# A channel-attention and FFN kernel: held subtractions of low halves, other rooms, and a tenth tile on seven products

## The chip, the cores and the metric

One core of a Trainium2 chip runs the whole program. The metric is the device time of one execution in microseconds (us); the times of several executions are given as a median with the lowest and the highest.

## What is computed

The reference attends over channels and then applies a two-layer network to every token.

```python
B, N, C = 4, 6080, 256            # d_model 256, d_ff 2048, 24320 tokens
qn = q / (norm(q, axis=1) + 1e-06)
kn = k / (norm(k, axis=1) + 1e-06)
s = kn.transpose(0, 2, 1) @ qn / tau
a = softmax(s)                    # over the last axis, 256 x 256 for each batch
x = (v @ a).reshape(B * N, C)
h = x @ w_in
g = maximum(0.01 * h, h)
out = g @ w_out
```

## The kernel before

**Tiles and slots.** For each batch the kernel multiplies the 256 x 256 attention matrix into `w_in` once, so that a token needs two projections: v by that product (256 to 2048), the leaky unit, and `w_out` (2048 to 256). The tokens are cut into 24 tiles of 2 x 512 or 2 x 496 tokens, six for each of four batches, and the 2048 hidden channels into eight pairs of 128-channel blocks. A tile and a pair make a slot, written (tile, pair) here: 192 slots, run one after the other by the loop over `i` and `p` at the end of the program. Operands are split into a high and a low half (float16 from tile 6 on); a product is three matmuls, or passes: high by high, low weight by high, high weight by low.

**The first projection** uses seven block products in place of eight (`block_product`, L1188, 21 matmuls in each slot, L1193). They accumulate in two PSUM banks, `ps_x` and `ps_z`. ScalarE copies partial sums out of `ps_x` (`taken`, tile `h`, L1239) or into `ps_z` (`seed`, L1228), and VectorE adds a copy to what stands in `ps_z` (`add`, tile `h`, L1233). The last product into `ps_x` waits for the copy `h22`, and the last into `ps_z` for VectorE's sum `h22`.

**The leaky unit** (`leaky`, L1199) works on the four blocks C11, C22, C21 and C12 of a slot. ScalarE writes the result in float32 (tile `g`, L1207) and its high half (tile `g_split`, L1207 or L1214); VectorE then subtracts the one from the other for the low half (L1218). C12 of a slot is handled at the start of the next one (`last`).

**The second projection** of a plain tile (`ffn_out`, L1598, matmuls at L1613) is a generator of 24 matmuls a pair: four blocks, two halves of the output, three passes. It runs one slot later, a few matmuls at a time: `out(6)`, `out(5)`, `out(7)` and `out(24)` fill the places in which TensorE would wait. After the last pair the four output banks are copied (L1630 on ScalarE, L1634 on VectorE) and stored.

**Fast tiles.** From tile 15 on (`FAST`, which `EARLY = 3` sets) a slot is written by `fast_slot` (L1514), and the second projection uses seven products as well: 21 matmuls a pair (`fast_out`, L1339). The sums of blocks that this needs are made by accumulating DMAs on POOL's queue (`sums_start`, L1305), the sums of `w_out` beforehand by VectorE (`wo_sums`, started in the slots of `SUMS_AT`). The first fast tile has its own rooms (`front` and `end`).

**Order of the rest.** All other work stands in queues (`todo`): splitting v for the next tile (`v_split`), squares and norms of q and k, scaled q and k (`unit` by VectorE, their high half `qk_split` by ScalarE, L362), the softmax, and the products and splits of the next batch's weights (`w_first`, `w_rest`, which POOL's queue stores). `slot(queue, room)` issues entries at its place until their lengths, constants in the code, fill the room. So the order on every engine is fixed when the program is built, and each engine runs it in order. A few lines of a plain slot show the places:

```python
                slot("dve", 2.1)
                block_product(i, p, x, S2, "T2", False, False)
                h12 = leaky(i, p, "C11", z if h11 is None else h11, lambda: taken(i, x))
                slot("dve", 2.2)
                slot("act", 1.8)
                out(5)
                block_product(i, p, z, S1, "T1", True, False)
                slot("pe", 1)
...
            block_product(i, p, x, S3, "T3", False, False)
            h22 = taken(i, x)
            add(i, h22, z)
```

Of the kernel before, what the change touches and what calls it, by code (L numbers as in the profile page):

```python
# [30 lines left out]
RBUFS = 4  # L31
RSQRT_MAGIC = float(0x5F3759DF)
TOP = 12
SUMS_AT = (79, 110, 113, 121)
UNITS = 5
SCORES_AT = {1: (8, 20), 2: (48, 22), 3: (0, 0)}
NORMS_AT = 80
G_SCALE = 2.0**-19
G_LESS = 2.0**-2
EARLY = 3  # L40


@with_exitstack
def channel_attention_ffn(
# [17 lines left out]
    nc = tc.nc  # L62
# [1133 lines left out]
                )  # L1196
        issued["pe"] = mm

    def leaky(i, p, name, h, then=None):  # L1199

        n = widths[i % NT]
        out = work.tile([P, TW], F32, name="g", bufs=3)
        sp = work.tile([P, 2, TW], pair_type(i), name="g_split", bufs=GBUFS)
        g_split[i, p, name] = sp

        def unit(to):
            return nc.scalar.activation(  # L1207
                out=to, in_=h[:, 0:n], func=AF.Prelu, alpha=0.01, scale=G_SCALE if i >= T16 else 1.0
            )

        run("act", unit, out[:, 0:n])
        between = then() if then else None
        if name == "C21" or then:
            run("act", lambda: nc.scalar.copy(out=sp[:, 0, 0:n], in_=out[:, 0:n]))  # L1214
        else:
            run("act", unit, sp[:, 0, 0:n])
        with in_order("dve"):
            issued["dve"] = nc.vector.tensor_tensor(  # L1218
                out=sp[:, 1, 0:n], in0=out[:, 0:n], in1=f32(sp[:, 0, 0:n]), op=ALU.subtract
            )  # L1220
        return between

    def seed(i, p, x, z):

# [373 lines left out]
    def ffn_out(i, p):  # L1598

        b, t = divmod(i, NT)  # L1600
        n = widths[t]
        f2 = (p // 2) * FPC + p % 2
        f1 = f2 + 2
        assert {f2 // FPB, f1 // FPB} <= wo_done
        if p == 0:
            o_ps[i] = [[bank("o", 4) for _ in range(CH)] for _ in range(2)]
        for name, f, j in (("C11", f1, 0), ("C22", f2, 1), ("C21", f2, 0), ("C12", f1, 1)):
            sp = g_split.pop((i, p, name))
            early = name in ("C11", "C22")
            for h in range(CH):  # L1610
                for k, (x, y) in enumerate(((0, 0), (1, 0), (0, 1))):
                    with in_order("pe"):
                        issued["pe"] = nc.tensor.matmul(  # L1613
                            out=o_ps[i][j][h][:, 0:n],
                            lhsT=wo_lhsT(i, x, f, h),
                            rhs=sp[:, y, 0:n],
                            start=p == 0 and early and k == 0,
                            stop=p == NPAIR - 1 and not early and k == 2,
                        )
                    yield  # L1620
            if p == NPAIR - 1 and not early:
                n0 = b * N + begins[t] + j * n
                act, dve = (nc.scalar.copy, nc.scalar), (nc.vector.tensor_copy, nc.sync)
                parts = [(0, 0, n, act[0], nc.sync), (1, 0, n, *dve)]
                for h, a, z, copy, queue in parts:
                    o = work.tile([P, TW], F32, name="o_sb", tag="temp", bufs=TEMPS)
                    if i < T16:
                        copy(out=o[:, a:z], in_=o_ps[i][j][h][:, a:z])
                    elif copy is act[0]:
                        nc.scalar.activation(  # L1630
                            out=o[:, a:z], in_=o_ps[i][j][h][:, a:z], func=AF.Copy, scale=v_scale[i].out
                        )
                    else:
                        nc.vector.tensor_scalar(  # L1634
                            out=o[:, a:z], in0=o_ps[i][j][h][:, a:z], scalar1=v_scale[i].out, scalar2=None,
                            op0=ALU.mult,
                        )
                    queue.dma_start(out=outT[h * P:(h + 1) * P, n0 + a:n0 + z], in_=o[:, a:z])

# [797 lines left out]
    for i in range(NTILES):  # L2439
        for p in range(NPAIR):  # L2440
# [17 lines left out]
            h11 = seed(i, p, x, y) if seeded else taken(i, x)  # L2458
            if seeded:
                z = y  # L2460
                if last is not None:
                    leaky(*last)
                    last = None
                slot("act", 0.65)
                slot("act_late", 0.65)
                out(6)
                slot("pe", 1 if len(todo["pe"]) < 2 else 3)
                block_product(i, p, z, A12, "B21", h11 is not None, True)
                if h11 is not None:
                    add(i, h11, z)  # L2470
                slot("dve", 2.1)
                block_product(i, p, x, S2, "T2", False, False)
                h12 = leaky(i, p, "C11", z if h11 is None else h11, lambda: taken(i, x))
                slot("dve", 2.2)
                slot("act", 1.8)
                out(5)
                block_product(i, p, z, S1, "T1", True, False)
                slot("pe", 1)
            else:
                block_product(i, p, y, A12, "B21", True, True)  # L2480
                slot("act", 0.65 if i else 0.75 if p else 1.5)
                slot("act_late", 0.65)
                add(i, h11, y)
                if last is not None:
                    leaky(*last)
                    last = None
                slot("dve", 1.45 if i else 1.3)
                out(5)
                slot("pe", 1 if i and len(todo["pe"]) < 2 else 3)
                if i:  # L2490
                    leaky(i, p, "C11", h11)
                slot("dve", 2.2 if i else 2.6 if p < NPAIR - 1 else 1.5)
                block_product(i, p, x, S2, "T2", False, False)
                h12 = taken(i, x)
                if i == 0:
                    leaky(i, p, "C11", h11)
                    slot("dve", 1.0)
                if i:
# [3 lines that stand above are left out]
                slot("pe", 1 if i or p else 2)  # L2502
# [2 lines left out]
            add(i, h22, z)  # L2505
            if i == 0:
                slot("act", 2.2)
            slot("dve", 1.45 if i else 2.8)
            out(7 if seeded else 8)
            slot("act_first", 0.65)  # L2510
# [2 lines left out]
            if i == 0:  # L2513
                slot("act", 0.6)
            else:
                leaky(i, p, "C22", h22)
            block_product(i, p, x, A22, "T4", False, True)
            block_product(i, p, z, S4, "B22", False, True)
            add(i, h12, z)
            leaky(i, p, "C21", x)  # L2520
            slot("act", 0.65 if i else 0.75)
            slot("act_late", 0.65)
            slot("dve", 0.8)
            if i == 0:
                leaky(i, p, "C22", h22)
                slot("dve", 1.5)
            if i == 0 and p < NPAIR - 1 or seeded and (i, p) != (FAST[0] - 1, NPAIR - 1):
                last = i, p, "C12", h12
            else:
                leaky(i, p, "C12", h12)  # L2530
            out(24)
            outs.append(ffn_out(i, p))
    while outs:
        out(24)
    fast_finish()
# [30 lines left out]
```

## Time and profile before

| | |
|---|---|
| median of 3 runs | 2066.24 us (2065.58 to 2069.65) |
| profiled execution, its own time | 2066.94 us |
| its span, first to last instruction | 2065.2 us |
| TensorE matmuls | 2037.5 us busy, 99% of the span, 9522 instructions |
| VectorE | 1658.5 us, 80%, 3077 instructions |
| ScalarE | 1547.5 us, 75%, 2866 instructions |
| GpSimd (POOL) | 338.2 us, 16%, 431 instructions |
| SyncE's DMA queue | 218.61 MB; GpSimd's DMA queue 112.29 MB |

Busy time is the time in which an engine runs at least one instruction. Matmuls are pipelined: each is shown with its own duration, longer than the distance to the next one. Idle time is put down to the instruction or the DMA that ended it. Tiles are found in the trace by the matmuls of L1193, 21 to a slot: tile 3 starts at 342.92 us, tile 13 at 1233.87, tile 14 at 1323.81, tile 15 at 1406.26, tile 16 at 1473.11, tile 17 at 1543.88, and the last slot at 2038.41.

### The profile page before, as it was taken

The page shows a single profiled execution, that of the slowest core. Times are in us where ns is not written, and L with a number is a line of the kernel's source. Part 1 is how long each engine was busy: PE and PEld are TensorE (multiplying, and loading weights), DVE is VectorE, ACT ScalarE, POOL GpSimd, SP SyncE. Part 2 cuts the span into 40 slices and gives each one's busy share as a digit, 9 for nine tenths or more (in the row PEclk, how much of TensorE's full clock was granted, in tenths as well). Part 3 has the DMA queues.
Part 4 walks back from the last instruction along what each step waited for, and adds up shares of the span by engine and source line. Part 5 has one row for each costly group of instructions (what it writes and reads, how often), then busy time and mean ns, then how long its engine had stood idle before and what let it go on. Part 6 is the DMA issues. An engine that isn't in the chain of part 4 may idle for free.

```text
span 2065.2 us, 27833 instructions
## 1 busy us (share of the span) xinstructions
PE 2037.5 (99%) x9522; PEld 1180.9 (57%) x9522; DVE 1658.5 (80%) x3077; ACT 1547.5 (75%) x2866; POOL 338.2 (16%) x431
## 2 busy tenths in 40 slices
PE   9999999999999999999999999999999999999999
PEld 8888887888874545444454554444444444444444
DVE  8987788776767787778787776877989889988976
ACT  6577777765567888877676666767988888898886
POOL 0000000000001222111010000102433333333342
PEclk9999999999999999999999999999999999999999
DMA  9945577445745877534233322213768876876774
GB/s 368 395 169 202 198 242 233 164 165 171 231 155 184 262 191 200 153 95 124 89 128 109 124 63 63 107 37 82 148 141 175 173 160 130 164 143 140 143 134 94
DMA packets 146815, 332.88 MB, mean 161 GB/s; under 512 B 16848, under 2 KB 48336, under 8 KB 146672
## 3 DMA queue, kind: packets, MB, share of 16 engines
q1 hardware_dynamic: 92912, 218.61, 31.3%
q0 software_dynamic: 53536, 112.29, 27.0%
q8 instruction: 75, 1.23, 0.2%
q14 instruction: 68, 0.56, 0.1%
q10 hardware_dynamic: 224, 0.20, 0.0%
HBM read 188.74 MB, written 57.42 MB: 119 GB/s over the span
## 4 chain that ended last, share of the span: by engine, by line
PE 87%; DVE 6%; ACT 4%; issue 2%; DMA 1%; POOL 0%; SPq 0%; ACTq 0%; POOLq 0%
PE ps_o L1613 25%; PE ps_x L1193 21%; PE ps_z L1193 16%; PE ps_o L1339 10%; PE ps_s L404 4%; PE ps_s L1339 2%; PE ps_y L1339 2%; PE ps_o L404 2%; DVE g_split L1218 1%; DVE h L1233 1%; PE ps_s L1965 1%; ACT g_split L1214 1%; PE ps_y L404 1%; ACT h L1239 1%; DVE v_split L1139 1%
## 5 line engine op out<-in xcount | busy, mean ns | idle before, releaser
L1613 PE MATMUL ps_o<-g_split,w_out_split 128*128 128x512 f16 (+3 forms) x2880 | 709.2, 382 | 0.2 <-ACT o_sb L1630 0.2
L1193 PE MATMUL ps_x<-v_split,w_split 128*128 128x512 f16 (+3 forms) x2280 | 619.7, 380 | 9.2 <-ACT h L1239 7.8
L1218 DVE TENSOR_TENSOR g_split<-g,g_split 128x512 f16<-128x512 f32 (+3 forms) x480 | 328.2, 684 | 239.4 <-ACT g_split L1207 171.6
L1193 PEld LDWEIGHTS <-w_split 128*128 128x128 f16 x3024 | 293.1, 98 | 367.3 <-issue 35.0
L1193 PE MATMUL ps_z<-v_split,w_split 128*128 128x512 f16 (+3 forms) x1704 | 463.3, 380 | 12.0 <-DVE h L1233 9.0
L1233 DVE TENSOR_TENSOR h<-ps_z,h 128x512 f32<-128x512 f32 (+1 forms) x387 | 263.8, 682 | 73.6 <-ACT h L1239 62.6
L1239 ACT COPY h<-ps_x 128x512 f32<-128x512 f32 (+1 forms) x395 | 229.0, 580 | 102.5 <-PE ps_x L1193 92.2
L1613 PEld LDWEIGHTS <-w_out_split 128*128 128x128 f16 x1728 | 168.9, 98 | 202.1 <-issue 1.0
L1207 ACT ACTIVATE g<-h 128x512 f32<-128x512 f32 (+1 forms) x250 | 156.9, 627 | 119.9 <-DVE h L1233 119.8
L1613 PEld LDWEIGHTS ps_o<-g_split,w_out_split 128*128 128x128 f32 x1152 | 216.4, 188 | 43.7
L1298 DVE TENSOR_TENSOR g_pair<-g_b,g_pair 128x512 f16<-128x512 f32 (+1 forms) x214 | 139.2, 678 | 45.9 <-ACT g_pair L1293 45.6
L1339 PE MATMUL ps_o<-g_pair,w_out_split 128*128 128x512 f16 (+1 forms) x630 | 172.8, 376 | 0.4 <-ACT g_pair L1293 0.3
L1207 ACT ACTIVATE g_split<-h 128x512 f16<-128x512 f32 (+3 forms) x248 | 152.2, 614 | 0.0
L1214 ACT CAST g_split<-g 128x512 f16<-128x512 f32 (+3 forms) x232 | 143.1, 617 | 3.7
L1339 PEld LDWEIGHTS <-spare 128*128 128x128 f16 x840 | 82.2, 98 | 96.9 <-issue 0.4
L1293 ACT CAST g_pair<-g_b 128x512 f16<-128x512 f32 (+1 forms) x214 | 123.1, 610 | 0.0
L1193 PEld LDWEIGHTS ps_x<-v_split,w_split 128*128 128x128 f32 x576 | 107.7, 188 | 25.6 <-ACT h L1239 2.7
L1207 ACT ACTIVATE g<-ps_z 128x512 f32<-128x512 f32 (+1 forms) x110 | 65.0, 591 | 64.8 <-PE ps_z L1193 64.3
L1228 ACT COPY ps_z<-ps_x 128x512 f32<-128x512 f32 (+1 forms) x110 | 62.5, 569 | 55.4 <-PE ps_x L1193 45.7
L1339 PEld LDWEIGHTS <-w_out_split 128*128 128x128 f16 x630 | 61.6, 98 | 72.9 <-issue 0.6
L1305 POOL DMA_DIRECT2D g_a<-g_a x70 | 63.3, 905 | 227.7 <-DVE g_pair L1298 140.1
L1298 DVE TENSOR_TENSOR g_pair<-g_a,g_pair 128x512 f16<-128x512 f32 (+1 forms) x144 | 97.2, 676 | 1.5 <-ACT g_pair L1293 1.0
(280 smaller groups left out, 2811.9 us busy)
## 6 DMA issues: line engine op xcount, KB each, us to landing
w_split<-w_dram SPq DMA_DIRECT2D x40, 896.0 KB, 6.9
qk_raw<-in_q_dram SPq DMA_DIRECT2D x115, 256.0 KB, 3.2
qk_raw<-in_k_dram SPq DMA_DIRECT2D x115, 256.0 KB, 5.8
v_raw<-in_vT_dram SPq DMA_DIRECT2D x32, 512.0 KB, 4.1
out_dram<-o_sb SPq DMA_DIRECT2D x64, 256.0 KB, 3.0
w_split<-w_dram SPq DMA_DIRECT2D x32, 448.0 KB, 5.2
spare<-spare POOLq DMA_DIRECT2D x23, 512.0 KB, 5.5
g_a<-g_a POOLq DMA_DIRECT2D x40, 256.0 KB, 3.3
```

Source lines behind the costliest of these rows:

```text
L404: mm = nc.tensor.matmul(out=out, lhsT=lhsT, rhs=rhs, start=start, stop=stop, skip_group_check=True)
L1193: mm = nc.tensor.matmul(out=ps[:, 0:n], lhsT=w[:, x, a, :], rhs=sp[:, y, 0:n], start=first and k == 0, stop=k == 2, skip_group_check=True,)
L1207: return nc.scalar.activation(out=to, in_=h[:, 0:n], func=AF.Prelu, alpha=0.01, scale=G_SCALE if i >= T16 else 1.0)
L1214: run("act", lambda: nc.scalar.copy(out=sp[:, 0, 0:n], in_=out[:, 0:n]))
L1218: issued["dve"] = nc.vector.tensor_tensor(out=sp[:, 1, 0:n], in0=out[:, 0:n], in1=f32(sp[:, 0, 0:n]), op=ALU.subtract)
L1233: issued["dve"] = nc.vector.tensor_tensor(out=h[:, 0:n], in0=ps[:, 0:n], in1=h[:, 0:n], op=ALU.add)
L1239: issued["act"] = nc.scalar.copy(out=h[:, 0:n], in_=ps[:, 0:n])
L1293: return nc.scalar.copy(out=sp[:, 0, 0:n], in_=g32[i, p, HELD.get(name, name)][:, 0:n])
L1298: return nc.vector.tensor_tensor(out=sp[:, 1, 0:n], in0=g32[i, p, HELD.get(name, name)][:, 0:n], in1=sp[:, 0, 0:n], op=ALU.subtract)
L1305: return nc.gpsimd.dma_start(out=g32[i, p, to][:, 0:n], in_=g32[i, p, of][:, 0:n], accum_op=ALU.add)
L1339: issued["pe"] = nc.tensor.matmul(out=ps[:, 0:n], lhsT=fast_lhsT(i, p, prod, x), rhs=sp[:, y, 0:n], start=p == 0 and k == 0, stop=ends and ...
L1613: issued["pe"] = nc.tensor.matmul(out=o_ps[i][j][h][:, 0:n], lhsT=wo_lhsT(i, x, f, h), rhs=sp[:, y, 0:n], start=p == 0 and early and k == ...
```

## The change

`leaky` gets an argument `held`: VectorE's subtraction is then put into a list (`rests`) and issued by `rest_of(n)` at a later place. In plain tiles from tile 1 on, C11's is issued behind the sum `h22`, C22's behind the sum `h12`, C21's at the start of the next slot and C12's behind the product T2 of that next slot. The rooms of a plain slot change: 1.8 to 1.3 and 0.65 to 1.25 for ScalarE, 0.8 to 1.45 for VectorE, and a room of 0.8 more at the end of each tile's first slot. In `ffn_out` the last matmul of a block and what follows it (the output copies) are issued in one step. `EARLY` becomes 4, so that tile 14 is the first fast tile, and three entries of `SUMS_AT` move up by eight slots.

```diff
-SUMS_AT = (79, 110, 113, 121)
+SUMS_AT = (79, 102, 105, 113)
...
-EARLY = 3
+EARLY = 4
...
-    def leaky(i, p, name, h, then=None):
+    def leaky(i, p, name, h, then=None, held=False):
...
-        with in_order("dve"):
-            issued["dve"] = nc.vector.tensor_tensor(
+        def rest():
+            return nc.vector.tensor_tensor(
                 out=sp[:, 1, 0:n], in0=out[:, 0:n], in1=f32(sp[:, 0, 0:n]), op=ALU.subtract
             )
+
+        if held:
+            rests.append(rest)
+        else:
+            run("dve", rest)
         return between
+
+    rests = []
+
+    def rest_of(n):
+        for _ in range(min(n, len(rests))):
+            run("dve", rests.pop(0))
...
@@ ffn_out
-                    yield
+                    if (h, k) != (CH - 1, 2):
+                        yield
...
                     queue.dma_start(out=outT[h * P:(h + 1) * P, n0 + a:n0 + z], in_=o[:, a:z])
+            yield
...
@@ the loop over slots
             if seeded:
                 z = y
+                rest_of(9 if p == 0 else 1)
                 if last is not None:
-                    leaky(*last)
+                    leaky(*last, held=True)
                     last = None
...
                 block_product(i, p, x, S2, "T2", False, False)
-                h12 = leaky(i, p, "C11", z if h11 is None else h11, lambda: taken(i, x))
+                rest_of(1)
+                h12 = leaky(i, p, "C11", z if h11 is None else h11, lambda: taken(i, x), held=True)
                 slot("dve", 2.2)
-                slot("act", 1.8)
+                slot("act", 1.3)
...
             add(i, h22, z)
             if i == 0:
                 slot("act", 2.2)
+            if seeded:
+                rest_of(9)
             slot("dve", 1.45 if i else 2.8)
...
-                leaky(i, p, "C22", h22)
+                leaky(i, p, "C22", h22, held=True)
             block_product(i, p, x, A22, "T4", False, True)
             block_product(i, p, z, S4, "B22", False, True)
             add(i, h12, z)
-            leaky(i, p, "C21", x)
-            slot("act", 0.65 if i else 0.75)
+            if i and p == 0 and 0.0:
+                pass
+            else:
+                rest_of(9)
+            leaky(i, p, "C21", x, held=i > 0)
+            slot("act", (1.25 if p else 1.25) if i else 0.75)
             slot("act_late", 0.65)
-            slot("dve", 0.8)
+            slot("dve", (1.45 if p else 1.45) if i else 0.8)
...
             else:
+                rest_of(9)
                 leaky(i, p, "C12", h12)
             out(24)
             outs.append(ffn_out(i, p))
+            if i and p == 0:
+                rest_of(9)
+                slot("dve", 0.8)
```

The first place is VectorE in slot (12, 4), from the second subtraction of the slot to the sum `h22` and a little past it. Before (`g_split` with its number names the block: 11481 is C12 of slot (12, 3), 11514 is C11 of this slot):

```order
L1218 TENSOR_TENSOR g_split_11481<-g_11480,g_split_11481 128x512
L1136 TENSOR_SCALAR v_split_11506<-v_raw_10960,v_scale_11145 128x512
L1139 SCALAR_TENSOR_TENSOR v_split_11506<-v_raw_10960,v_scale_11145,v_split_11506 128x512
L1160 TENSOR_TENSOR v_raw_10960<-v_raw_10960 128x512
L1218 TENSOR_TENSOR g_split_11514<-g_11513,g_split_11514 128x512
L1160 TENSOR_TENSOR v_raw_10960<-v_raw_10960 128x512
L366 TENSOR_TENSOR qk_split_11463<-unit_11430,qk_split_11463 128x2x256
L356 TENSOR_TENSOR unit_11522<-qk_raw_11190,spare_5885 128x512
L1233 TENSOR_TENSOR h_11542<-ps_z_11475,h_11542 128x512
L356 TENSOR_TENSOR unit_11545<-qk_raw_11268,spare_5885 128x512
```

The same engine and place in the change (11537 is C21 of slot (12, 3), 11560 its C12, 11593 is C11 of this slot):

```order
L1218 TENSOR_TENSOR g_split_11537<-g_11536,g_split_11537 128x512
L1136 TENSOR_SCALAR v_split_11584<-v_raw_11041,v_scale_11227 128x512
L1139 SCALAR_TENSOR_TENSOR v_split_11584<-v_raw_11041,v_scale_11227,v_split_11584 128x512
L1160 TENSOR_TENSOR v_raw_11041<-v_raw_11041 128x512
L1218 TENSOR_TENSOR g_split_11560<-g_11559,g_split_11560 128x512
L1160 TENSOR_TENSOR v_raw_11041<-v_raw_11041 128x512
L366 TENSOR_TENSOR qk_split_11540<-unit_11509,qk_split_11540 128x2x256
L356 TENSOR_TENSOR unit_11600<-qk_raw_11304,spare_5885 128x512
L1244 TENSOR_TENSOR h_11615<-ps_z_11553,h_11615 128x512
L1218 TENSOR_TENSOR g_split_11593<-g_11592,g_split_11593 128x512
```

The kinds of instructions ahead of the sum (L1233, now L1244) are the same; each subtraction's place is taken by the block before it, and C11's has moved behind the sum.

The second place is VectorE in slot (13, 6), between the first subtraction and the sum `h22`. Before:

```order
L874 SCALAR_TENSOR_TENSOR w_first<-w_s,w_first 128x256 x2
L1218 TENSOR_TENSOR g_split<-g,g_split 128x512
L1975 TENSOR_TENSOR w_c<-w_c,ps_y 128x512
L1136 TENSOR_SCALAR v_split<-v_raw,v_scale 128x512
L1139 SCALAR_TENSOR_TENSOR v_split<-v_raw,v_scale,v_split 128x512
```

And in the change:

```order
L1136 TENSOR_SCALAR v_split<-v_raw,v_scale 128x512
L1139 SCALAR_TENSOR_TENSOR v_split<-v_raw,v_scale,v_split 128x512
L874 SCALAR_TENSOR_TENSOR w_first<-w_c,w_first 128x128
L874 SCALAR_TENSOR_TENSOR w_first<-w_c,w_first 128x256
L1218 TENSOR_TENSOR g_split<-g,g_split 128x512
L874 SCALAR_TENSOR_TENSOR w_first<-w_s,w_first 128x256 x2
```

The splits of the last batch's weights (L874) stand closer here: twelve instructions in the whole slot in place of six. Before, the last of them stood in slot (14, 1).

## Rows read from the trace of the kernel before

**Rows 1.** The page's first part: busy time of each engine.

```profile
PE 2037.5 (99%) x9522; PEld 1180.9 (57%) x9522; DVE 1658.5 (80%) x3077; ACT 1547.5 (75%) x2866; POOL 338.2 (16%) x431
```

**Rows 2.** Busy time by stretch: tiles 3-13, 14, 15, 16, 17 to last slot.

```profile
core 0: us, PE busy (x) PEld busy (x) DVE busy (x) ACT busy (x) POOL busy (x), PEclk, DMA share, GB/s
...
342.92:1323.81 980.89, 964.86 (x4596) 563.11 (x4595) 744.79 (x1407) 699.80 (x1321) 89.92 (x134) 1.00 0.49 149
1323.81:1406.26 82.45, 78.62 (x362) 35.22 (x361) 60.25 (x119) 55.74 (x108) 6.13 (x9) 1.00 0.14 52
1406.26:1473.11 66.85, 65.79 (x298) 28.95 (x297) 56.69 (x108) 56.73 (x104) 21.54 (x25) 1.00 0.63 126
1473.11:1543.88 70.77, 70.77 (x338) 32.87 (x337) 64.17 (x120) 60.99 (x115) 26.76 (x32) 1.00 0.71 138
1543.88:2038.41 494.53, 493.52 (x2314) 226.26 (x2313) 433.04 (x787) 424.61 (x786) 189.54 (x221) 1.00 0.75 150
```

**Rows 3.** Waits of TensorE in tiles 3 to 13: us, times, longest.

```profile
PE ps_x L1193 <- ACT h L1239: 7.4, 8, 1.6
PE ps_z L1193 <- DVE h L1233: 7.4, 17, 1.1
PE ps_x L1193 <- ACT wo L1007: 0.5, 1, 0.5
PE ps_o L1613 <- ACT o_sb L1630: 0.2, 1, 0.2
```

**Rows 4.** Busy time by stretch: slots (7, 4), (7, 5) and (14, 6).

```profile
738.39:749.51 11.12, 11.12 (x54) 5.70 (x53) 9.28 (x16) 9.69 (x19) 2.50 (x4) 1.00 0.55 136
749.51:761.18 11.67, 11.30 (x54) 5.67 (x53) 9.29 (x16) 9.70 (x19) 3.38 (x5) 1.00 0.81 196
...
1386.83:1396.54 9.71, 9.71 (x46) 4.41 (x45) 4.56 (x8) 6.49 (x12) 0.00 (x0) 1.00 0.19 74
```

**Rows 5.** Order of time, TensorE in slot (12, 4): start, duration, instruction, idle before.

```profile
1192.50 0.81 PE L1193 MATMUL ps_z<-v_split,w_split 128*128 128x512 f16 x3
...
1193.79 1.67 PE L1613 MATMUL ps_o<-g_split,w_out_split 128*128 128x512 f16 x7
1196.44 0.81 PE L1193 MATMUL ps_x<-v_split,w_split 128*128 128x512 f16 x3 [0.97 <-ACT h L1239]
...
1197.81 1.46 PE L1613 MATMUL ps_o<-g_split,w_out_split 128*128 128x512 f16 x6
```

**Rows 6.** Order of time, ScalarE in slot (12, 4).

```profile
1195.28 0.62 ACT L362 CAST qk_split<-unit 128x512 f16<-128x512 f32 x1 [2.56 <-DVE unit L356]
1195.81 0.58 ACT L1239 COPY h<-ps_x 128x512 f32<-128x512 f32 x1
```

**Rows 7.** Order of time, VectorE in slots (12, 4) and (12, 5).

```profile
1189.71 0.69 DVE L1218 TENSOR_TENSOR g_split<-g,g_split 128x512 f16<-128x512 f32 x1 [0.64 <-ACT g_split L1207]
...
1192.75 0.69 DVE L1218 TENSOR_TENSOR g_split<-g,g_split 128x512 f16<-128x512 f32 x1 [0.56 <-ACT g_split L1214]
...
1196.42 0.69 DVE L1233 TENSOR_TENSOR h<-ps_z,h 128x512 f32<-128x512 f32 x1 [1.17 <-ACT h L1239]
...
1202.06 0.69 DVE L1218 TENSOR_TENSOR g_split<-g,g_split 128x512 f16<-128x512 f32 x1 [1.25 <-ACT g_split L1207]
...
1204.98 0.69 DVE L1218 TENSOR_TENSOR g_split<-g,g_split 128x512 f16<-128x512 f32 x1 [0.91 <-ACT g_split L1214]
...
1207.98 0.68 DVE L1233 TENSOR_TENSOR h<-ps_z,h 128x512 f32<-128x512 f32 x1
```

**Rows 8.** Waits of VectorE in tiles 3 to 13: us, times, longest.

```profile
DVE g_split L1218 <- ACT g_split L1207: 125.1, 108, 2.4
DVE g_split L1218 <- ACT g_split L1214: 58.8, 63, 3.5
DVE h L1233 <- ACT h L1239: 35.8, 36, 2.1
```

**Rows 9.** Waits of TensorE in tile 14.

```profile
PE ps_z L1193 <- ACT ps_z L1228: 2.4, 1, 2.4
PE ps_z L1193 <- DVE h L1233: 1.4, 3, 0.7
```

**Rows 10.** Order of time, ScalarE in slot (14, 1).

```profile
1337.04 0.61 ACT L862 ACTIVATE w_first<-w_c 128x128 f16<-128x128 f32 x2 [2.57 <-DMA w_dram<-w_first]
```

## The prediction

> **What bounds the kernel now.** I read the page's engine totals first, then the same totals cut into stretches, then TensorE's waits in two of the stretches, then the order of time around one wait. A reader should see five things.
>
> TensorE is busy 99% of the span [rows 1] at a granted clock of 1.00, which is its level of 2.4 GHz [rows 2]. VectorE (80%) and ScalarE (75%) are not far behind. The end is therefore set by TensorE: its work, plus the time that the others make it wait.
>
> The waits lie in a few places [rows 2]. Tiles 3 to 13 take 980.89 us, with TensorE busy 964.86: 16.03 us idle. Tile 14 loses 3.83 us, tile 15 1.06, tile 16 none, and the 494.53 us from tile 17 to the start of the last slot 1.01. In tiles 3 to 13, 17 waits are for VectorE's sum `h` and 8 for ScalarE's copy `h`, with two others: 27 waits, 15.5 us [rows 3].
>
> A wait costs more than its idle time. Two slots of the same matmuls (54 in each) last 11.12 and 11.67 us; the second has only 0.37 us of idle [rows 4]. The other 0.18 us is the draining tail of the matmul before the wait, which counts as busy. So tiles 3 to 13 lose about 16.0 + 27 x 0.18 = 20.9 us. Tile 14 is checked directly: its quiet slots take 9.71 us [rows 4], eight would be 77.7, and it took 82.45: 4.8 us.
>
> The Trainium skill ("Trainium Kernel Development and Optimization", Performance Expectations) says that matmul busy time is a bad measure of the distance to the limit because matmuls are pipelined. The trace agrees: by busy time the two stretches lose 19.9 us, by slot lengths 25.7. The sum below goes by the slot lengths.
>
> Why TensorE waits is seen in slot (12, 4). The last product into `ps_x` waits 0.97 us for ScalarE's copy `h` [rows 5]. ScalarE had stood 2.56 us before that copy, for a `unit` that VectorE makes [rows 6]. VectorE had stood 0.64 and then 0.56 us in front of two subtractions at L1218, whose high half ScalarE had not finished [rows 7]: 1.20 us, against a loss of 0.97 + 0.18. In slot (12, 5) two such stands of 1.25 and 0.91 us come ahead of VectorE's sum at 1207.98 [rows 7]. Over tiles 3 to 13 VectorE stands 183.9 us before such subtractions [rows 8], some 2.1 us in each of 88 slots; what reaches TensorE is a ninth of that.
>
> **The change, part by part.**
>
> *Seven products in tile 14.* The second projection of a fast tile takes 21 matmuls a pair where a plain one takes 24: 24 fewer over eight pairs. Seven matmuls are shown with 1.67 us and three with 0.81 [rows 5], so one more costs 0.215 us: **-5.2 us**, on TensorE itself. ScalarE and VectorE get what before's tile 15 already gives them, and POOL 32 more accumulating DMAs. In the new order tile 14 holds before's tile 15 and tile 15 holds before's tile 16, instruction for instruction on ScalarE and VectorE but for widths and one deferred subtraction. Tile 15 lost 1.06 us of idle with those instructions and tile 16 none, at the same 32 POOL DMAs and VectorE 64.17 us busy of 70.77 [rows 2]. So I charge the new tile 14 with what tile 15 loses now, and the new tile 15 with nothing. What falls out is the plain tile 14 with its waits [rows 9]: **-4.8 us**. Its greatest, 2.4 us, came from ScalarE standing 2.57 us for the DMA that empties a `w_first` buffer [rows 10].
>
> *Held subtractions.* No instruction is added. The number of VectorE instructions ahead of the sum `h22` stays as it was in (12, 4); what changes is which blocks' subtractions stand there. Those of C22, C21 and C12 of the slot before take the places of C21, C12 and this slot's C11, whose high halves ScalarE finishes only just then. The stands go; the work stays. Upper bound of the gain: all 20.9 us. Lower bound: zero, if other stands take their place, and below zero if the subtractions come late (a rival). The row nearest to it is (12, 4), where the stands ahead equal the loss; in (12, 5) they are 2.16 us against a loss near 0.55. But the waits for ScalarE hang on a longer chain, and the softmax and weight steps bring stands of their own. I take three quarters: **-16 us**.
>
> Is a held half late? The shortest lead is C11's: in (12, 4) it would follow the sum of 1196.42 [rows 7] and end near 1197.8. TensorE's third pass over C11 comes in the next slot, after the six matmuls from 1197.81, three of the next product and two passes, near 1200.2 [rows 5]: 2.4 us in hand.
>
> *Rooms and sums.* The rooms move steps between places of the same slot: no count changes, and the price lies in the three quarters. `SUMS_AT` moves three groups of weight sums up by eight slots, and the weight steps of the last batch, which ran in tiles 13 and 14, now end in tile 13. In (13, 6) VectorE gets twelve `w_first` instructions where it had six. Between zero and tile 14's 4.8 us can come back here; I take it as part of the quarter that stays.
>
> *Output copies* stand right behind their last matmul instead of at the next group: one wait of 0.2 us in tiles 3 to 13 [rows 3] can go; counted at nothing.
>
> Sum: -5.2 - 4.8 - 16 = -26.0. The profiled execution took 2066.94 us (span 2065.2 and 1.7 around it), 0.7 above the median of the three runs. 2066.94 - 26.0 = **2041 us**.
>
> **Rivals.**
>
> *ScalarE's chain holds.* If the stands on L1218 only hide ScalarE's own lateness, the eight waits for its copy stay (7.4 + 8 x 0.18 = 8.8 us) and half of the rest: 6 us instead of 16, so 2051. For it: VectorE also stood 35.8 us for that copy [rows 8]. Against: in (12, 4) ScalarE stood for VectorE, not the other way.
>
> *The squeezed steps wait in tile 13.* The `w_first` buffer wait and its neighbours return one tile earlier and take back the 4.8 us: 2046. For it: the wait hangs on buffers that a DMA empties, and the steps are denser. Against: tile 14 held them while its quiet slots left VectorE 4.56 us busy of 9.71 [rows 4], so it was order rather than load that stalled it.
>
> *Late halves (the slower side).* VectorE runs so far behind that TensorE meets held halves unfinished. Each such meeting stops it once a slot; the 104 plain slots of tiles 1 to 13 eat the 26 us at 0.25 us a slot. At 0.3 us it is 2066.94 - 26 + 31 = 2072. It needs VectorE to trail by the 2.4 us lead, which at 744.79 us busy of 980.89 [rows 2] only a few slots could see.
>
> *Blocked POOL DMAs.* If VectorE's instructions held up POOL's issues, tile 14's pair sums would come late. In tile 16 the same mix leaves POOL 26.76 us busy in 32 issues, of 70.77, and TensorE without idle [rows 2]. POOL would set the pace only if each issue's 0.84 us grew by more than 44 / 32 = 1.4 us; at three times the length it would be 80 us, 9.5 more than the tile: 2050.5. Against it stands tile 16 itself. The Trainium skill ("SBUF — State Buffer", SBUF: two separate sides, with the section on the bandwidth pool behind it) states such a lock between VectorE's two-port modes and the descriptors that GpSimd writes: 620 ns for a DMA alone, 3100 ns beside VectorE. An estimate by that page is 2.5 us more for each of 32, and so some 2077 us in all. The trace of tile 16 disagrees with it for this mix.
>
> **How the numbers follow.** Forecast 0.75, ScalarE's chain 0.09, squeezed steps 0.10, late halves 0.05, blocked DMAs 0.01. From no change a measurement tells 0.2%, 4.1 us. All but the late halves are faster, save 0.01 of the squeezed steps (several tiles hit) that ends within 0.2%; late halves near the break-even give another 0.01. That makes 0.94, 0.02, 0.04. The range: with all 20.9 us gone 2036, and 2034 with the small waits outside these tiles as well; upward it takes in 2046 and 2051 and ends at 2053. That leaves out some 0.15.
>
> **What would show it.** TensorE's matmul records fall by 24, and tile 14 is near 67 us with waits like tile 15's. Right: VectorE's idle before the subtraction falls from 183.9 us to a small part in tiles 3 to 13, and TensorE's idle there from 16 to about 4. Wrong: that idle falls but TensorE's stays (ScalarE's chain); waits gather in tile 13 on `w_first` or `ps_z`; the second projection's matmuls `ps_o` wait for `g_split`; or tile 14 shows waits beyond tile 15's.

## The result and the profile after

The changed kernel takes **2034.95 us** (median of 4 runs, 2034.52 to 2035.84); the kernel before took 2067.36 us beside it (4 runs). The ratio is 0.9843, with an interval of 0.9826 to 0.986. The forecast was 2041 us, 2034 to 2053, so the time lies 0.95 us above the lower end of the range. One execution of a kernel below, C11's behind the room, took 7555.62 us where its three others took 2036.05 to 2037.11; it is left out of that kernel's median, and its cause is not known.

The profiled execution of the change took 2034.65 us, its span 2032.8: 32.4 us less than the span of before.

The page's first part answers to [rows 1]. There are 24 matmuls fewer, and every engine's share is higher because the span is shorter:

```profile
PE 2022.6 (99%) x9498; PEld 1180.1 (58%) x9498; DVE 1665.4 (82%) x3115; ACT 1564.8 (77%) x2890; POOL 367.1 (18%) x463
```

The busy time by stretch answers to [rows 2] (same columns): tiles 3 to 13, 14, 15, 16, and 17 to the start of the last slot.

```profile
342.03:1302.32 960.29, 957.19 (x4596) 564.27 (x4595) 746.29 (x1442) 710.02 (x1338) 97.86 (x143) 1.00 0.51 155
1302.32:1369.17 66.85, 65.78 (x298) 28.98 (x297) 57.11 (x109) 56.50 (x104) 21.80 (x25) 1.00 0.62 126
1369.17:1441.70 72.53, 72.53 (x337) 32.84 (x336) 65.22 (x120) 62.38 (x115) 26.56 (x31) 1.00 0.70 137
1441.70:1512.47 70.77, 70.77 (x338) 32.87 (x336) 64.15 (x120) 61.03 (x115) 27.40 (x32) 1.00 0.74 146
1512.47:2006.00 493.53, 493.34 (x2315) 226.19 (x2314) 433.04 (x787) 424.61 (x786) 189.22 (x221) 1.00 0.75 150
```

Set against [rows 2], tiles 3 to 13 give 980.89 - 960.29 = 20.6 us. Tiles 14 and 15 together go from 149.3 to 139.4: 9.9 us. From tile 16 to the last slot it is 1.0 us (565.3 to 564.3). The remaining 0.9 us lies ahead of tile 3, which starts at 342.03 in place of 342.92. The clock is 1.00 in all of them, in both kernels.

What TensorE still waits for in tiles 3 to 13 answers to [rows 3]: 4 waits where there were 27.

```profile
PE ps_x L1193 <- ACT h L1250: 0.9, 1, 0.9
PE ps_y L348 <- DVE n_split L341: 0.8, 1, 0.8
PE ps_z L1193 <- DVE h L1244: 0.7, 1, 0.7
PE ps_z L1193 <- ACT ps_z L1239: 0.6, 1, 0.6
```

VectorE's waits in the same stretch answer to [rows 8]. The 183.9 us before subtractions have become 8.6. VectorE now stands before its sums (L1244, L1233 before), for ScalarE's copy or for TensorE's product, because it comes there early:

```profile
DVE h L1244 <- ACT h L1250: 149.0, 75, 5.0
DVE h L1244 <- PE ps_z L1193: 25.9, 28, 2.5
DVE g_split L1218 <- ACT g_split L1207: 8.6, 9, 1.8
```

Slot (12, 4) shows how, against [rows 5 to 7]. On VectorE the subtraction of C12 starts at once; the step `unit` follows; then the engine stands 1.54 us before the sum `h22`; C11's subtraction comes behind it.

```profile
1175.94 0.68 DVE L1218 TENSOR_TENSOR g_split<-g,g_split 128x512 f16<-128x512 f32 x1
...
1177.74 0.68 DVE L356 TENSOR_TENSOR unit<-qk_raw,spare 128x512 f32<-128x512 f32 x1
1179.97 0.69 DVE L1244 TENSOR_TENSOR h<-ps_z,h 128x512 f32<-128x512 f32 x1 [1.54 <-ACT h L1250]
1180.58 0.68 DVE L1218 TENSOR_TENSOR g_split<-g,g_split 128x512 f16<-128x512 f32 x1
```

ScalarE's cast waits 0.38 us for that `unit`, where it stood 2.56 us before [rows 6], and its copy `h22` now waits for TensorE:

```profile
1178.46 0.62 ACT L362 CAST qk_split<-unit 128x512 f16<-128x512 f32 x1 [0.38 <-DVE unit L356]
1179.35 0.59 ACT L1250 COPY h<-ps_x 128x512 f32<-128x512 f32 x1 [0.27 <-PE ps_x L1193]
```

TensorE goes on to the last product into `ps_x` without a pause, where it lost 0.97 us before [rows 5]:

```profile
1179.15 1.67 PE L1624 MATMUL ps_o<-g_split,w_out_split 128*128 128x512 f16 x7
1180.66 0.81 PE L1193 MATMUL ps_x<-v_split,w_split 128*128 128x512 f16 x3
```

### The profile page after: what moved, and what is told of

Its sections match the earlier page's. It is cut to its first block, busy times and chain, and to the rows that moved or that the text cites. A ratio compares the mean times of both kernels' runs of the same rounds, so it can differ in the third digit from the quotient of the medians.

```text
span 2032.8 us, 27944 instructions
## 1 busy us (share of the span) xinstructions
PE 2022.6 (99%) x9498; PEld 1180.1 (58%) x9498; DVE 1665.4 (82%) x3115; ACT 1564.8 (77%) x2890; POOL 367.1 (18%) x463
## 4 chain that ended last, share of the span: by engine, by line
PE 96%; DVE 2%; DMA 1%; ACT 0%; issue 0%; SPq 0%; DVEq 0%; ACTq 0%; POOLq 0%
PE ps_o L1624 28%; PE ps_x L1193 24%; PE ps_z L1193 18%; PE ps_o L1350 12%; PE ps_s L404 4%; PE ps_y L1350 2%; PE ps_s L1350 2%; PE ps_o L404 2%; PE ps_s L1978 1%; PE ps_y L404 1%; DMA w_dram<-w_first 1%; PE ps_y L1978 0%; PE ps_y L821 0%; PE ps_o L1373 0%; DVE g_split L1218 0%; DVE h L1244 0%
## 5 line engine op out<-in xcount | busy, mean ns | idle before, releaser
L1624 PE MATMUL ps_o<-g_split,w_out_split 128*128 128x512 f16 (+3 forms) x2688 | 661.9, 382 | 0.0
L1244 DVE TENSOR_TENSOR h<-ps_z,h 128x512 f32<-128x512 f32 (+1 forms) x387 | 264.5, 683 | 228.0 <-ACT h L1250 192.5
L1218 DVE TENSOR_TENSOR g_split<-g,g_split 128x512 f16<-128x512 f32 (+3 forms) x448 | 302.1, 678 | 16.0 <-ACT g_split L1207 15.6
L1624 PEld LDWEIGHTS <-w_out_split 128*128 128x128 f16 x1536 | 150.3, 98 | 178.7
L1207 ACT ACTIVATE g<-h 128x512 f32<-128x512 f32 (+1 forms) x234 | 146.8, 627 | 75.0 <-DVE h L1244 75.0
L1309 DVE TENSOR_TENSOR g_pair<-g_b,g_pair 128x512 f16<-128x512 f32 (+1 forms) x238 | 155.0, 679 | 49.2 <-ACT g_pair L1304 48.8
L1350 PE MATMUL ps_o<-g_pair,w_out_split 128*128 128x512 f16 (+1 forms) x702 | 192.9, 376 | 0.4 <-ACT g_pair L1304 0.3
L1207 ACT ACTIVATE g_split<-h 128x512 f16<-128x512 f32 (+3 forms) x232 | 142.4, 614 | 0.0
L1304 ACT CAST g_pair<-g_b 128x512 f16<-128x512 f32 (+1 forms) x238 | 137.1, 611 | 0.0
L1214 ACT CAST g_split<-g 128x512 f16<-128x512 f32 (+3 forms) x216 | 133.3, 617 | 3.5
L1350 PEld LDWEIGHTS <-w_out_split 128*128 128x128 f16 x702 | 68.6, 98 | 81.5 <-issue 0.6
L1309 DVE TENSOR_TENSOR g_pair<-g_a,g_pair 128x512 f16<-128x512 f32 (+1 forms) x160 | 108.1, 676 | 1.7 <-ACT g_pair L1304 1.1
L1207 ACT ACTIVATE g<-ps_z 128x512 f32<-128x512 f32 (+1 forms) x102 | 60.3, 591 | 60.7 <-PE ps_z L1193 60.4
```

Of the source, the lines that this page charges most:

```text
L1207: return nc.scalar.activation(out=to, in_=h[:, 0:n], func=AF.Prelu, alpha=0.01, scale=G_SCALE if i >= T16 else 1.0)
L1218: return nc.vector.tensor_tensor(out=sp[:, 1, 0:n], in0=out[:, 0:n], in1=f32(sp[:, 0, 0:n]), op=ALU.subtract)
L1244: issued["dve"] = nc.vector.tensor_tensor(out=h[:, 0:n], in0=ps[:, 0:n], in1=h[:, 0:n], op=ALU.add)
L1304: return nc.scalar.copy(out=sp[:, 0, 0:n], in_=g32[i, p, HELD.get(name, name)][:, 0:n])
L1309: return nc.vector.tensor_tensor(out=sp[:, 1, 0:n], in0=g32[i, p, HELD.get(name, name)][:, 0:n], in1=sp[:, 0, 0:n], op=ALU.subtract)
L1350: issued["pe"] = nc.tensor.matmul(out=ps[:, 0:n], lhsT=fast_lhsT(i, p, prod, x), rhs=sp[:, y, 0:n], start=p == 0 and k == 0, stop=ends and ...
```

## The experiments

Theory A says that VectorE's stands before the subtractions (its idle time in front of them) cause TensorE's waits. Theory B says that the new rooms do the work, and the hold only moves the stands. Twelve kernels ran in three sessions; the kernel before took 2065.91, 2066.41 and 2066.40 us in them.

| kernel | us, median | ratio to before (interval) | tiles 3 to 13, us |
|---|---|---|---|
| held subtractions alone | 2041.91 | 0.9886 (0.987 to 0.9903) | 959.50 |
| rooms alone | 2065.10 | 0.9998 (0.9989 to 1.0007) | 984.71 |
| tile 14 fast alone | 2056.12 | 0.9951 (0.9936 to 0.9966) | 980.47 |
| change, all subtractions at once | 2056.69 | 0.9954 (0.994 to 0.9969) | 981.36 |
| change, C11's at once | 2051.73 | 0.9927 (0.9911 to 0.9944) | 977.97 |
| change, C11's alone held | 2038.78 | 0.9865 (0.9851 to 0.988) | 965.20 |
| change, C21's and C12's late | 2156.71 | 1.0438 (1.0422 to 1.0453) | 1062.79 |
| change, the same two one place later | 2037.21 | 0.9858 (0.9843 to 0.9873) | 963.21 |
| change, C11's behind the room | 2036.16 | 0.9852 (0.9832 to 0.9871) | 961.73 |
| change, least rooms | 2035.52 | 0.9849 (0.9834 to 0.9863) | 961.27 |
| change, old output copies | 2036.79 | 0.9854 (0.984 to 0.9869) | 962.78 |
| change once more | 2035.13 | 0.9845 (0.9831 to 0.986) | 960.40 |

### Held subtractions alone

Everything of the change but the hold is taken back:

```diff
-EARLY = 4
+EARLY = 3
-SUMS_AT = (79, 102, 105, 113)
+SUMS_AT = (79, 110, 113, 121)
-                slot("act", 1.3)
+                slot("act", 1.8)
-            slot("act", (1.25 if p else 1.25) if i else 0.75)
+            slot("act", 0.65 if i else 0.75)
-            slot("dve", (1.45 if p else 1.45) if i else 0.8)
+            slot("dve", 0.8)
-                slot("dve", 0.8)
...
```

> The kernel before with the held subtractions alone (old rooms, nine fast tiles, old place of the output copies). Theory A, that VectorE's stands before the subtractions cause TensorE's waits: tiles 3 to 13 fall from 980.9 us to 960 to 964, tiles 1 and 2 by about 1, tile 14 keeps its wait behind the w_dram store; in all 19 to 24 us less than before, ratio 0.988 to 0.991. Theory B, that the new rooms carry half or more: tiles 3 to 13 stay above 970, in all less than 12 us. VectorE's idle before the subtractions falls to a small part under both.

It ran 24.0 us faster than before. Its tiles 3 to 13:

```profile
341.73:1301.23 959.50, 957.12 (x4596) 564.42 (x4595) 730.66 (x1406) 701.09 (x1321) 90.58 (x134) 1.00 0.50 153
```

That is the whole gain of these tiles, 0.8 us more than in the change, and half a microsecond below the 960 to 964 that theory A expected. Tile 14, still plain here, took 79.47 us in place of 82.45. So theory A holds and B falls.

### Rooms alone

`leaky` issues each subtraction at once; nine fast tiles, old copies.

```diff
-        if held:
+        if False:
             rests.append(rest)
...
-EARLY = 4
+EARLY = 3
...
```

> The kernel before with the new rooms alone (and the room added at the end of each tile's first slot); each subtraction is issued at once, as before. Theory A: tiles 3 to 13 stay within 5 us of 980.9, VectorE still stands more than 150 us before the subtractions there; in all within 6 us of before. Theory B: 10 us or more less than before, from tiles 3 to 13.

The time is that of before. In tiles 3 to 13 VectorE stands 106.9 us for halves written at L1207 and 60.3 us for those of L1214: 167.2 us, nearly as before. In all, the rooms by themselves are worth nothing. That is a sum of two parts that happen to cancel in the profiled execution: tiles 3 to 13 took 3.8 us more than before (984.71), and tile 14 took 3.1 less (79.32), without the wait of 2.4 us [rows 9].

### Tile 14 fast, subtractions at once

The kernel before with three edits. VectorE's wider room is one of them, on the reading of the code that with 0.8 us a split of v for tile 15 would not be issued before that tile needs it. No kernel with the narrow room was run, so this is not shown.

```diff
-SUMS_AT = (79, 110, 113, 121)
+SUMS_AT = (79, 102, 105, 113)
-EARLY = 3
+EARLY = 4
-            slot("dve", 0.8)
+            slot("dve", 1.45 if i else 0.8)
```

> The kernel before with tile 14 fast and the three groups of sums moved up, and of the rooms only VectorE's 0.8 to 1.45 in plain tiles; subtractions issued at once. By the terms of the prediction: tiles 14 and 15 together fall from 149.3 us to 139 to 140, the rest stays; in all 8 to 12 us less, ratio 0.994 to 0.996. Rival, squeezed steps: tile 13 grows by 3 us or more over its 89.9 with waits behind weight steps, and in all only 3 to 7 us less.

9.8 us faster. Tiles 3 to 13, then tiles 14 and 15 together:

```profile
343.10:1323.57 980.47, 963.41 (x4596) 563.45 (x4595) 758.27 (x1438) 705.26 (x1336) 95.14 (x141) 1.00 0.49 151
1323.57:1463.17 139.60, 138.47 (x635) 61.81 (x633) 123.28 (x232) 119.62 (x220) 49.77 (x59) 1.00 0.68 138
```

The pair costs 139.6 us against 149.3, and tile 13 took 87.27 us, less than its 89.93 of before. No wait behind the squeezed steps is seen here. The two gains alone, 24.0 and 9.8, add to 33.8 us; together they gave 32.4 beside the first measurement of before and 31.3 (2066.40 - 2035.13) in the last session. The 3.0 us that the hold saves in a plain tile 14 stand in both gains, which would make 30.8; the rest is not accounted for, and the medians of before differ by 1.5 us among sessions.

### The change with every subtraction at once

```diff
-        if held:
+        if False:
             rests.append(rest)
```

> The changed kernel with each subtraction issued at once, all else new. Theory A: tiles 3 to 13 take 976 to 982 us again, with VectorE standing more than 150 us before the subtractions; in all 2053 to 2060 us, about 10 less than before, ratio 0.993 to 0.997. Theory B: tiles 3 to 13 at 970 or less and in all 2046 or less.

2056.69 us, tiles 3 to 13 at 981.36, and VectorE stands 162.6 us before subtractions there: without the hold, all that is left is the gain of tile 14. It is the other half of the first experiment.

### Which subtraction it is

Two kernels part the four. In the first, C11's is issued at once and the three others are held:

```diff
-                h12 = leaky(i, p, "C11", ..., lambda: taken(i, x), held=True)
+                h12 = leaky(i, p, "C11", ..., lambda: taken(i, x))
```

> The changed kernel with C11's subtraction issued at once, so that it stands ahead of the sum h22 again; the other three stay held. Theory A1, the stand nearest to the sum is the one that reaches TensorE: tiles 3 to 13 rise from 960.3 us to 972 or more, in all 2046 us or more. Theory A2, each of the four stands counts alike: tiles 3 to 13 near 965, in all 2038 to 2042. Theory A3, it is the stands of the other blocks: within 2 us of the changed kernel's 2035.

In the second, C11's alone is held:

```diff
-                    leaky(*last, held=True)
+                    leaky(*last)
-                leaky(i, p, "C22", h22, held=True)
+                leaky(i, p, "C22", h22)
-            leaky(i, p, "C21", x, held=i > 0)
+            leaky(i, p, "C21", x)
```

> The changed kernel with C11's subtraction alone held; C22's, C21's and C12's are issued at once. A1: tiles 3 to 13 at 966 us or less, in all 2041 or less. A2: near 976, in all 2048 to 2054. A3: near 980, in all 2053 to 2057.

Theory A1 holds. With C11's alone held, tiles 3 to 13 lose 981.36 - 965.20 = 16.2 us of the 21.1 that all four give; the three others alone are worth 981.36 - 977.97 = 3.4. How long VectorE stands does not tell this. Its waits in tiles 3 to 13, C11's at once:

```profile
DVE g_split L1218 <- ACT g_split L1214: 91.7, 75, 2.4
DVE h L1244 <- PE ps_z L1193: 41.0, 44, 2.8
DVE h L1244 <- ACT h L1250: 40.4, 35, 2.1
DVE g_split L1218 <- ACT g_split L1207: 10.3, 11, 1.8
```

and C11's alone held:

```profile
DVE h L1244 <- ACT h L1250: 123.6, 70, 5.0
DVE g_split L1218 <- ACT g_split L1207: 73.7, 85, 2.2
```

The second kernel keeps 73.7 us of stands and is 4.9 us longer there than the change; the first has 102.0 us of them and is 17.7 us longer. What differs is what is queued behind the stand, and slot (12, 4) of the first kernel shows the whole chain. ScalarE makes C11's high half behind the copy of T2, at 1189.17, and VectorE stands 1.40 us for it. Three steps follow the subtraction, `unit` last, and the sum stands behind ScalarE's copy:

```profile
1187.74 0.68 DVE L1218 TENSOR_TENSOR g_split<-g,g_split 128x512 f16<-128x512 f32 x1
1189.83 0.69 DVE L1218 TENSOR_TENSOR g_split<-g,g_split 128x512 f16<-128x512 f32 x1 [1.40 <-ACT g_split L1214]
...
1191.64 0.69 DVE L356 TENSOR_TENSOR unit<-qk_raw,spare 128x512 f32<-128x512 f32 x1
1193.50 0.69 DVE L1244 TENSOR_TENSOR h<-ps_z,h 128x512 f32<-128x512 f32 x1 [1.17 <-ACT h L1250]
```

ScalarE has the cast of that `unit` ahead of its copy `h22`, and stands 2.57 us:

```profile
1189.17 0.62 ACT L1214 CAST g_split<-g 128x512 f16<-128x512 f32 x1
1192.36 0.62 ACT L362 CAST qk_split<-unit 128x512 f16<-128x512 f32 x1 [2.57 <-DVE unit L356]
1192.88 0.58 ACT L1250 COPY h<-ps_x 128x512 f32<-128x512 f32 x1
```

and TensorE, whose product for that copy is the first line here, waits for the copy exactly as it did before [rows 5]:

```profile
1190.22 0.81 PE L1193 MATMUL ps_x<-v_split,w_split 128*128 128x512 f16 x3
...
1193.52 0.81 PE L1193 MATMUL ps_x<-v_split,w_split 128*128 128x512 f16 x3 [0.97 <-ACT h L1250]
```

So a wait that the view puts down to ScalarE's copy is the same stand of VectorE, passed on through the cast. The Trainium skill ("PSUM — Partial Sum Buffer", Engine vs sequencer instructions) says that the queues of ScalarE and VectorE are strictly first in, first out. The rows agree: the copy stands behind the cast, although its product ended near 1191.0 on TensorE, 1.3 us before the cast began.

### C11's subtraction behind the room

Is it the subtraction ahead of the sum that costs, or the steps queued behind the stand? Here it stays ahead of the sum, but those steps go first.

```diff
                 slot("dve", 2.2)
+                rest_of(9)
                 slot("act", 1.3)
```

> The changed kernel with C11's subtraction still ahead of the sum h22, but behind the room of 2.2 (two to four other steps) in place of ahead of it. Theory C1, what costs is the work queued behind the stand: ScalarE has the half ready by then, TensorE's waits stay gone, within 4 us of the changed kernel. Theory C2, any subtraction of the running slot ahead of the sum costs: 2045 us or more, VectorE still stands more than 40 us for C11's half.

Theory C1 holds: the time is 1.0 us above the change of the same session, and the intervals overlap. In slot (12, 4) `unit` now comes 5.51 us after the start of the slot (1174.73), as in the change (1177.74 after 1172.23), and not 7.70 as in the kernel just shown (1191.64 after 1183.94). C11's subtraction finds its half ready:

```profile
1180.24 0.69 DVE L356 TENSOR_TENSOR unit<-qk_raw,spare 128x512 f32<-128x512 f32 x1
1180.84 0.69 DVE L1218 TENSOR_TENSOR g_split<-g,g_split 128x512 f16<-128x512 f32 x1
1182.47 0.69 DVE L1244 TENSOR_TENSOR h<-ps_z,h 128x512 f32<-128x512 f32 x1 [0.94 <-ACT h L1250]
```

VectorE still stands 34.4 us for C11's halves in tiles 3 to 13, less than the 40 that theory C2 asked for, with nothing but the sum behind it; that stretch is 961.73 us, 1.3 above the change of the same session (960.40). The edit takes away both most of these stands (91.7 us with C11's at once) and the work behind them, so it does not price the two apart; but the stands fell to 0.4 of what they were and the cost from 17.7 us to 1.3.

### Held too far

C21's and C12's subtractions go behind the next slot's sum:

```diff
-                rest_of(9 if p == 0 else 1)
+                rest_of(9 if p == 0 else 0)
...
-                rest_of(1)
+                rest_of(0)
                 h12 = leaky(i, p, "C11", ...
```

> The changed kernel with C21's and C12's subtractions held further, behind the sum h22 of the next slot. In slot (12, 4) the sum ends at 1180.66, so C21's low half would end near 1181.3, and TensorE's pass over it stands at about 1179.8: a wait of some 1.4 us at the second projection in each of 104 slots, in all 100 to 160 us more than the changed kernel's 2035 (2135 to 2195). Rival, TensorE is that far behind VectorE in most slots: less than 30 us more.

121.8 us above the change. The view of TensorE's waits over the whole run names it, and a slot of tile 12 shows it: four matmuls of the second projection stop for the low half.

```profile
PE ps_o L1624 <- DVE g_split L1218: 106.0, 78, 2.8
```

```profile
1287.04 0.81 PE L1624 MATMUL ps_o<-g_split,w_out_split 128*128 128x512 f16 x3
1289.20 1.02 PE L1624 MATMUL ps_o<-g_split,w_out_split 128*128 128x512 f16 x4 [1.35 <-DVE g_split L1218]
```

The wait is as long as worked out (1.36 us of idle on the mean), but it falls in 78 slots, six to a tile, not in 104: the first two slots of a tile are spared, for the code empties the list of held subtractions at the start and at the end of a tile's first slot. With the drain it costs 121.8 / 78 = 1.56 us each time. The rival "late halves" of the prediction was thus a real mechanism with a real price; the change stays clear of it.

A second kernel holds the two by one place less: C21's behind T2, C12's behind the sum.

```diff
-                rest_of(9 if p == 0 else 1)
+                rest_of(9 if p == 0 else 0)
```

> The changed kernel with C21's subtraction one place later (behind the product T2 of the next slot) and C12's behind the sum h22: one subtraction fewer ahead of that sum. By the working of slot (12, 4) C21's low half is then some 3 us early and C12's some 0.6 to 1.2 us early, so nothing waits for them: within 2 us of the changed kernel's 2035, up to 2.5 us less if the waits left in tiles 3 to 13 hang on VectorE's queue. Rival, C12's half comes late in many slots: 5 us or more above, with waits at the second projection for the low half.

2037.21 us: 2.3 above the change's first measurement, 2.1 above its later one, just outside the 2 us expected, and with overlapping intervals. No wait for a low half is listed, so the rival's cause is not there; tiles 3 to 13 took 963.21 us, and the few waits there are for the same things as in the change. One subtraction fewer ahead of the sum brings nothing more.

### The smaller edits

Least rooms: ScalarE's rooms and the output copies as before, no room behind the first slot.

```diff
-                slot("act", 1.3)
+                slot("act", 1.8)
-            slot("act", (1.25 if p else 1.25) if i else 0.75)
+            slot("act", 0.65 if i else 0.75)
-                slot("dve", 0.8)
...
```

> The changed kernel with ScalarE's old rooms (1.8 and 0.65), without the room at the end of each tile's first slot, and with the output copies at their old place; of the rooms only VectorE's 0.8 to 1.45 stays. If these edits carry nothing: within 2 us of the changed kernel in the same session; it could be up to 1 us faster, since tiles 3 to 13 took 959.5 us with all the old rooms and 960.3 with the new. If ScalarE's rooms matter: 4 us or more slower, with waits for ScalarE's copy.

Old copies: the step behind a block's last matmul is one group later again.

```diff
-                    if (h, k) != (CH - 1, 2):
-                        yield
+                    yield
...
-            yield
```

> The changed kernel with the output copies at their old place, one group of matmuls later. Counted at nothing in the prediction: within 1 us of the changed kernel in the same session. Rival: a wait for the output bank (ps_o for o_sb) returns in each tile, 0.2 to 0.8 us each, in all 2 us or more.

The change once more, for comparison:

> The changed kernel once more beside the three others: 2034 to 2036 us, ratio 0.984 to 0.986.

Least rooms and old copies stand 0.4 and 1.7 us above the change of the same session (2035.13), with ratios whose intervals overlap its own. For the rooms nothing can be told. With the old copies, expected within 1 us, two waits of 0.6 us in all for an output bank return. But the first of the two kernels has the old copies as well, with one such wait of 0.8 us, and costs only 0.4; so the 1.7 us cannot be laid to the copies, and they are not settled. No other kernel of the twelve beats the change.

## Why the prediction was right, and where it was off

**What bounds the kernel: right.** TensorE sets the end in both kernels, and the time is its work plus its waits.

**Seven products in tile 14 and its waits (-5.2 and -4.8): right.** Tiles 14 and 15 gave 9.9 us by their lengths, and 9.8 us in the kernel with that edit nearly alone. The new tile 14 took 66.85 us, as the old tile 15 did, with the same two listed waits of 0.4 and 0.3 us; the new tile 15 has no idle at all, with VectorE 65.22 us busy of 72.53. POOL was busy 26.56 us there against 26.76 in the old tile 16, and TensorE never waited for its sums. The lock that the Trainium skill ("SBUF — State Buffer", SBUF: two separate sides, with the section on the bandwidth pool behind it) states is one between VectorE's two-port modes and the descriptors that GpSimd writes, and its figures stand beside a `tensor_copy`. No such lock shows here; but 78 of VectorE's 119 instructions in that tile are `tensor_tensor`, and no run shows the mode of any, so this is no test of the page, and "disagrees" in the prediction says too much.

**Held subtractions (-16): the mechanism right, the term too small.** "I take three quarters" is the step that failed. Tiles 3 to 13 gave 20.6 us and tiles 1 and 2 another 1.25. By the spans 32.4 us went where the sum had 26.0: 9.9 in tiles 14 and 15, these two parts, and 1.0 from tile 16 on, less 0.4 ahead of tile 1; tiles 1 and 2 and those from 16 on had no term. Two reasons were given for the missing quarter. The first was that the waits for ScalarE's copy hang on a longer chain: they do, but the chain starts at the same stand, C11's, and passes through `unit` and its cast. [rows 6] had shown this link in one slot; the discount treated it as a cause of its own. The second was the softmax and weight steps: each of the four waits left stands behind such a step or one of the norms, and they cost 3.0 us of idle together. The time stayed in the range narrowly: its lower end had been reckoned with all 20.9 us gone, which is about what came.

**The upper bound of 20.9 us: too low.** 20.6 us went while 3.1 us of idle and four tails of 0.18 stay, which makes a loss of 24.4 us before. The bound added tails to the 27 listed waits. The trace has ten more stretches of idle there, too short for the list, whose tails would add some 1.8 us (an estimate, at 0.18 each); and delays shorter than the tail leave no idle at all. Tiles 1 and 2 show that, before:

```profile
178.27:260.44 82.17, 82.17 (x361) 67.34 (x360) 61.15 (x101) 62.55 (x116) 0.00 (x0) 1.00 0.63 211
260.44:342.92 82.48, 82.48 (x362) 67.18 (x360) 66.89 (x113) 61.44 (x114) 0.00 (x0) 1.00 0.69 225
```

and after:

```profile
178.63:260.43 81.80, 81.80 (x362) 67.51 (x360) 61.31 (x101) 62.72 (x116) 0.00 (x0) 1.00 0.62 206
260.43:342.03 81.60, 81.60 (x362) 67.59 (x360) 66.72 (x113) 61.73 (x114) 0.00 (x0) 1.00 0.69 233
```

TensorE is busy without a gap in all four, and yet the same 360 matmuls of each tile took 0.37 and 0.88 us longer before. Their starts show where: nearly all follow the one ahead by 0.23 us, but before 15 into `ps_z`, where the sums are read, follow by 0.28 to 0.34, which is 1.2 us more in all; after there are two, with 0.2 us. That busy time of matmuls is a bad measure, as the Trainium skill ("Trainium Kernel Development and Optimization", Performance Expectations) says, goes further than the prediction used it: even a slot without idle is not a quiet slot.

**Rooms, sums, copies (nothing): right** within what the runs tell. The squeezed steps do wait, but little. The one wait of tile 13, 0.60 us, is for a copy into `ps_z` that ScalarE makes behind a `w_first` step, and ScalarE had stood for the DMA that empties the buffer, as in [rows 10]:

```profile
1292.79 0.61 ACT L862 ACTIVATE w_first<-w_c 128x128 f16<-128x128 f32 x2 [1.22 <-DMA w_dram<-w_first]
1293.31 0.70 ACT L862 ACTIVATE w_first<-w_s 128x256 f16<-128x256 f32 x2
1293.92 0.57 ACT L1239 COPY ps_z<-ps_x 128x512 f32<-128x512 f32 x1
```

In the profile of the change once more it is 1.1 us; in tile 14 before it was 2.4 [rows 9]. Tile 13 is still 86.88 us long, 3.05 less than before.

**The rivals.** ScalarE's chain fell with the waits for its copy (7.4 us in eight to 0.9 in one). The squeezed steps came true in kind, at 0.6 to 1.1 us and not 4.8. Late halves and blocked DMAs did not occur in the change; the first was made to occur, at 1.56 us a meeting.

**What stays open.** Tile 18 is 0.85 us shorter after, with its instructions unchanged: a wait of 0.8 us for ScalarE is gone there, and the tile takes 72.71 us in every other kernel but the rooms alone, where it takes 73.68. So the hold alone and the tenth fast tile alone each take it away; no kernel was made to settle how.

## What to carry to other kernels

When an engine that runs in order stands for another, price the stand by what is queued behind it and by how soon the next handoff is due, not by its length alone: 73.7 us of stands cost 4.9 us here, and 102.0 cost 17.7. A step whose result is needed late and whose input comes late belongs behind the handoff; putting the steps that others wait for ahead of it does nearly as much. How far it may be held is read from the pass that uses it: one place further cost about 2 us at most, the next one 122.

## What had not been expected

TensorE loses time that leaves no idle in the record: 1.25 us in tiles 1 and 2, as shown above, and by the count of tiles 3 to 13 some 3.5 us more than the bound from the idle and the listed waits' tails (24.4 against 20.9), about half of it beside idle too short for the list. The length of like stretches shows it; the list of waits does not. And three gains that seemed apart (waits for VectorE's sum, for ScalarE's copy, and the small delays) came for the most part from one subtraction in each slot: C11's held alone gives 16.2 of the 21.1 us, and in tiles 1 and 2 all of the 1.25.
